# Attention's two column tiles in one step and one bank per l, where a batch's part has at most 256 tokens

## The chip, the cores and the metric

The kernel runs on one core of one Trainium2 chip. The metric is the device time of one execution in microseconds, as the median of several runs. The core's engines are named as the profile names them: PE is the tensor engine (PEld its weight loads), DVE the vector engine, ACT the scalar engine, POOL the GpSimd engine, SP the engine that issues most of the DMAs.

## The reference

A linear attention with a root-mean-square norm is followed by a two-layer network with a leaky ReLU. All data are float32; there are 8 batches of 576 tokens, 8 heads of 64, so 4608 rows of 512 for the network, whose inner width is 2048.

```python
kv = np.einsum('bhsd,bhse->bhde', k, v)
out = np.einsum('bhsd,bhde->bhse', q, kv)
rms = np.sqrt(np.mean(out * out, axis=-1, keepdims=True) + 1e-06)
attn_out = (out / rms * g_norm).astype(np.float32)

B, H, S, D = attn_out.shape                       # 8, 8, 576, 64
x = attn_out.transpose(0, 2, 1, 3).reshape(B * S, H * D)

h = x @ w_in                                      # 512 -> 2048
g = np.maximum(0.01 * h, h)
result = (g @ w_out).astype(np.float32)           # 2048 -> 512
```

## The kernel before

The network works in 9 blocks of 512 tokens, and a batch has 576. So batch b gives 512 - 64b tokens to block b and 64(b + 1) tokens to block b + 1: two parts, each with its own "tail" (`o = q kv`, then the norm). The first 512 tokens of batch 0 are made by code of their own at the start. The other fifteen parts go through the functions below. Parts with at most 256 tokens are the second ones of batches 0 to 3 (64, 128, 192, 256) and the first ones of batches 4 to 7 (256, 192, 128, 64).

Heads lie in pairs (`NP` = 4 pairs p, `l` the half of a pair), and a head's 64 output columns are split into two column tiles e of 32. For one e, eight matmuls fill the two tiles `o_ps[0]` and `o_ps[1]`: each uses 64 rows and 32 columns of the tensor engine's array, so eight of them fit beside one another. A float32 matmul is two instructions in the trace. The tile for the sum of squares, `sum0` or `sum1`, takes the squares of the first column tile directly; those of the second go to a buffer of `t2k` and are added.

```python
    ps_att = ctx.enter_context(tc.tile_pool(name="ps_att", bufs=2, space=bass.MemoryType.PSUM))
    ps_m = ctx.enter_context(tc.tile_pool(name="ps_m", bufs=1, space=bass.MemoryType.PSUM))

    pin = tc.keep_in_program_order
    steady = first_done = False

    def in_turn(ins):

        if steady:
            pin(ins)
# ... cut ...
    N2 = NT // 2                 # 256
# ... cut ...
    def t2k(n, name):
        home = {"tag": name, "bufs": 1} if name[:3] == "sum" else {"tag": "t2k", "bufs": 3}
        return work.tile([P, n], F32, name=name, **home)

    def x_of(lo, hi):
        return block(lo // NT)[:, :, lo % NT:lo % NT + hi - lo]

    def o_products(b, lo, hi, e, o_ps):
        for p in range(NP):
            for l in range(2):
                r = slice(64 * l, 64 * l + 64)
                matmul(o_ps[half_of(p, l)][E * p:E * p + E, :],
                       lhsT=kvs[b % 2][r, p, E * e:E * e + E],
                       rhs=qTs[b][r, p, lo - b * S:hi - b * S], start=True, stop=True)

    def outputs(b, lo, hi, e, sums):


        x, n = x_of(lo, hi), hi - lo
        o_ps = [ps_att.tile([P, n], F32, tag="att", name="o_ps") for _ in range(2)]
        o_products(b, lo, hi, e, o_ps)
        for l in range(2):
            sq = t2k(n, "sq" if e else f"sum{l}")
            nc.scalar.activation(sq, o_ps[l], func=AF.Square)
            if e == 0:
                sums.append(sq)
            else:
                in_turn(nc.vector.tensor_add(sums[l], sums[l], sq))
        for l in range(2):
            nc.scalar.activation(x[:, 2 * l + e, :], o_ps[l], func=AF.Copy, scale=g_sb[:, e:e + 1])
```

The tiles `o_ps` lie in `ps_att`, which has two banks. They are shared with the products of k and v of the next batch. `divide` turns the sums, takes root and reciprocal, spreads them and scales x; it is a generator, so that its pieces can be placed in different slots:

```python
    def divide(lo, hi, sums):

        x, n = x_of(lo, hi), hi - lo
        rms = work.tile([P, 2, n // E], F32, tag="rms", name="rms", bufs=2)
        for l in range(2):
            t = t2k(n, "turned")
            in_turn(nc.vector.transpose(t, sums[l]))
            in_turn(nc.vector.tensor_reduce(rms[:, l, :], t.rearrange("p (a i) -> p a i", i=E),
                                            axis=AX.X, op=ALU.add))
            if l:
                act = nc.scalar.activation(rms, rms, func=AF.Sqrt, scale=1.0 / D, bias=eps_sb)
                if first_done:
                    pin(act)
            yield
        in_turn(nc.vector.reciprocal(rms, rms))
        spread = []
        for l in range(2):
            t = t2k(n, "spread")
            nc.scalar.copy(t.rearrange("p (a i) -> p a i", i=E),
                           rms[:, l, :].unsqueeze(2).to_broadcast([P, n // E, E]))
            spread.append(t)
        yield
        for l in range(2):
            inv = t2k(n, "inv")
            in_turn(nc.vector.transpose(inv, spread[l]))
            to = x[:, 2 * l:2 * l + 2, :]
            in_turn(nc.vector.tensor_mul(to, to, inv.unsqueeze(1).to_broadcast([P, 2, n])))
            yield

    def tail_of(b, lo, hi, fine=False):
        sums = []
        for e in range(2):
            outputs(b, lo, hi, e, sums)
            yield
        for _ in divide(lo, hi, sums):
            if fine:
                yield
        if not fine:
```

From the third block on (`fine`), the steps of one batch are dealt out over the slots of a block's network, and the second part's first column tile comes between two pieces of the first part's norm:

```python
        # in attention(b, apart, fine): the two parts of a batch
        tails = [tail_of(b, max(i * NT, b * S), min((i + 1) * NT, (b + 1) * S), fine)
                 for i in (b, b + 1)]
        if not fine:
            for tail in tails:
                yield from tail
            return

        for tail in (0, 0, 0, 0, 0, 1, 0, 0, 1, 1, 1, 1, 1, 1):
            next(tails[tail])
            yield
```

The network's products are made by Strassen's method in seven steps. A slot has one step of the first product (`h_ha` and `h_hb`, or `h_hc` and `h_hd`, 8 + 6 matmul instructions), then what attention has for this slot, then one step of the second product (`o_a` or `o_c`, 8 instructions). Banks of `h` are added to and emptied in turn, so that a step writes a bank only after the scalar or the vector engine has taken out the one before it:

```python
            for t in range(7):
                slot = 7 * c + t
                go(h_steps, 1)
                if not one:
                    # ... cut ...
                    for _ in range(FINE_SLOTS.get(slot, 0)):
                        go(a_steps, 1)
                    # ... cut ...
                if slot in HELD and i == NB - 1:
                    pass
                elif waited == LAG:
                    go_o()
```

In the steps of block 2 and later (`steady`), the instructions of the vector engine go through `in_turn` and keep the order in which they are written; so do all matmuls, always. Those of the scalar engine may be put in another order when the program is built.

Of the kernel before, what the change touches and what calls it, by code (L numbers as in the profile page):

```python
# [9 lines left out]
F32 = mybir.dt.float32  # L10
U32 = mybir.dt.uint32
I64 = mybir.dt.int64
AF = mybir.ActivationFunctionType
# [10 lines left out]
def kernel(  # L24
# [36 lines left out]
    nc = tc.nc  # L61
    B, H, S, D = q.shape
    DM, DF = w_in.shape
    P = 128
# [7 lines left out]
    N2 = NT // 2  # L72
# [14 lines left out]
    ps_att = ctx.enter_context(tc.tile_pool(name="ps_att", bufs=2, space=bass.MemoryType.PSUM))  # L87
# [5 lines left out]
# [4 lines that stand above are left out]
# [20 lines left out]
    def matmul(*args, **kw):  # L117
        pin(nc.tensor.matmul(*args, **kw))  # L118
# [4 lines left out]
    def half_of(p, i):  # L123


        return i ^ (p & 1)
# [168 lines left out]
    g_sb = consts.tile([P, 2], F32, name="g_sb")  # L295
# [6 lines left out]
    def block(i):  # L302
        if i not in xTs:
            xTs[i] = xpool.tile([P, NE, NT], F32, tag="xT", name="xT")
        return xTs[i]
# [20 lines left out]
# [57 lines that stand above are left out]
            in_turn(nc.vector.tensor_mul(to, to, inv.unsqueeze(1).to_broadcast([P, 2, n])))  # L383
            yield

    def tail_of(b, lo, hi, fine=False):
        sums = []
        for e in range(2):
            outputs(b, lo, hi, e, sums)
            yield  # L390
        for _ in divide(lo, hi, sums):
            if fine:
                yield
        if not fine:
            yield

    def attention(b, apart=True, fine=False):
# [31 lines left out]
        if not apart:  # L429
            copy_kv(b, kv_ps)  # L430
# [4 lines that stand above are left out]
# [488 lines left out]

    first_attention()
    steps = {i: tail for tail in [tail_of(0, NT, S)] for i in (6, 8, 10)}
    a_steps = attention(1, False)
    steps.update((i, a_steps)
# [21 lines left out]
    x_sides, _, sums, _ = sides_x(1)  # L949
# [27 lines left out]
    for i in range(1, NB):  # L977
# [4 lines left out]
        for c in range(NC):  # L982
# [3 lines left out]
# [4 lines that stand above are left out]
# [7 lines left out]
                    if i + 1 < NB:  # L997
                        if slot == 20:
                            x_sides, new_quarters, sums, inner = sides_x(i + 1)
# [13 lines left out]
                if one:  # L1013
# [14 lines left out]
                    if slot == 24:  # L1028
                        go(a_steps)
                        x_sides, new_quarters, sums, inner = sides_x(i + 1)  # L1030
# [47 lines left out]
```

## Time and profile before

| what | value |
|---|---|
| median of 3 runs | 932.22 us (930.87 to 932.27) |
| span of the profiled run | 929.0 us, 17587 instructions |
| granted PE clock in the profiled run | 0.999 |
| o_ps matmuls on PE | x544, of these x64 at the start |
| Square into `sum` and `sq` on ACT | x30 and x30 |
| copies of o_ps into xT on ACT | x60 |
| additions of `sum` and `sq` on DVE | x30 |

The profile's page begins with each engine's busy time, its share of the span and its number of instructions. The chain that ended last is followed back from the last instruction, at each step to what released it; asked for in order of time, it lists start, length and what ran. In a list of waits each line has who waited, for whom, the total in us, how often, and the longest. In the timeline a line has start, length, engine, line of the code, operation, output and inputs, shape and count, and in brackets the idle time ahead of it. Some lines of the timeline name a helper: L118 is every matmul but a few, so there the tile's name tells what it is.

### The profile page before, as it was taken

How to read it: one execution, taken by the hardware profiler on the slowest of the kernel's cores; microseconds unless marked ns; L12 is line 12 of the kernel's file. 1: busy time of each engine (PE TensorE's matmuls, PEld its weight loads, DVE VectorE, ACT ScalarE, POOL GpSimd, SP SyncE). 2: the span in 40 equal slices, each digit the busy share in tenths (PEclk: the TensorE clock that was granted, in tenths of full speed). 3: DMA queues.
4: the chain of work that ended last, by engine and by line, in shares of the span. 5: the costliest groups of instructions: out<-in, count | busy, mean ns of one | idle time of the engine just before them, and what ended most of it. 6: DMA issues, size and time to landing. Idle time of an engine off the chain costs nothing.

```text
span 929.0 us, 17587 instructions
## 1 busy us (share of the span) xinstructions
PE 918.4 (99%) x6856; PEld 776.2 (84%) x6856; DVE 619.2 (67%) x998; ACT 331.0 (36%) x667; POOL 319.0 (34%) x318
## 2 busy tenths in 40 slices
PE   8999999999999999999999999999999999999997
PEld 5544447888998999899989999899988999999996
DVE  4866995586456876597756874687568744654554
ACT  4544632242134332532343423342343333223330
POOL 2000364977522532226211711272225322532222
PEclk9999999999999999999999999999999999999999
DMA  9999926895597679856995599658655676667632
GB/s 258 226 246 239 217 99 199 275 298 165 193 323 245 184 206 300 267 175 190 284 289 180 172 281 293 202 179 256 229 168 177 197 219 185 186 199 221 189 111 91
DMA packets 90066, 200.03 MB, mean 215 GB/s; under 512 B 9856, under 2 KB 42112, under 8 KB 89984
## 3 DMA queue, kind: packets, MB, share of 16 engines
q1 hardware_dynamic: 79392, 186.85, 68.5%
q10 hardware_dynamic: 10144, 10.88, 3.4%
q8 instruction: 55, 0.90, 0.4%
q0 software_dynamic: 448, 1.18, 0.3%
q14 instruction: 27, 0.22, 0.1%
HBM read 172.39 MB, written 26.48 MB: 214 GB/s over the span
## 4 chain that ended last, share of the span: by engine, by line
PE 95%; DMA 2%; DVE 2%; issue 0%; ACT 0%; POOL 0%; ACTq 0%; DVEq 0%; POOLq 0%
PE o_a L118 21%; PE o_c L118 21%; PE h_ha L118 11%; PE h_hb L118 8%; PE h_hc L118 8%; PE h_hd L118 6%; PE o_acc L118 6%; PE h_ps L118 6%; PE o_ps L118 2%; PE kv_ps L118 2%; PE h_a L118 1%; PE h_b L118 1%; DMA pairs<-in_v_dram 1%; PE h_c L118 1%; PE h_d L118 1%; DMA pairs<-in_moe_w_out_dram 1%
## 5 line engine op out<-in xcount | busy, mean ns | idle before, releaser
L589 POOL TENSOR_TENSOR gs<-g 128x512 f32<-128x512 f32 x64 | 81.3, 1289 | 442.9 <-ACT g L760 442.9
L589 DVE TENSOR_TENSOR o<-o_c,o 128x512 f32<-128x512 f32 x104 | 71.6, 689 | 111.8 <-PE o_c L118 111.8
L760 ACT ACTIVATE g<-g 128x512 f32<-128x512 f32 x124 | 78.2, 631 | 120.5 <-DVE g L589 120.5
L824 ACT COPY w_all<-h_ha 128x512 f32<-128x512 f32 x84 | 48.7, 580 | 187.9 <-PE h_ha L118 179.2
L589 DVE TENSOR_TENSOR o<-o_a,o 128x512 f32<-128x512 f32 x88 | 60.5, 687 | 68.0 <-PE o_a L118 67.9
L118 PE MATMUL o_c<-pairs,gs 128*128 128x256 f32 x384 | 91.3, 381 | 0.0
L118 PE MATMUL o_a<-pairs,gs 128*128 128x256 f32 x384 | 90.8, 379 | 0.0
L118 PEld LDWEIGHTS o_c<-pairs,gs 128*128 128x128 f32 x384 | 69.8, 190 | 9.3 <-issue 1.4
L118 PEld LDWEIGHTS o_a<-pairs,gs 128*128 128x128 f32 x384 | 69.8, 190 | 7.8
L118 PE MATMUL o_c<-w,g 128*128 128x256 f32 x256 | 61.6, 383 | 0.0
L118 PE MATMUL o_a<-w,g 128*128 128x256 f32 x256 | 61.6, 383 | 0.0
L118 PEld LDWEIGHTS h_ha<-stage,w_all 128*128 128x128 f32 x448 | 58.7, 192 | 2.8
L118 PE MATMUL h_ha<-stage,w_all 128*128 128x128 f32 x448 | 59.0, 275 | 0.0
L118 PE MATMUL h_ps<-xT,w_all 128*128 128x512 f32 (+1 forms) x136 | 57.9, 570 | 0.2 <-DVE w_all L255 0.2
L118 PE MATMUL o_acc<-w,g 128*128 128x512 f32 x128 | 58.0, 597 | 0.0
L589 DVE TENSOR_TENSOR g<-g,pairs 128x512 f32<-128x512 f32 x84 | 55.6, 689 | 1.9
L118 PEld LDWEIGHTS o_a<-w,g 128*128 128x128 f32 x256 | 46.4, 190 | 11.4 <-ACT pairs L824 2.7
L589 POOL TENSOR_TENSOR pairs<-w_all 128x512 f32<-128x512 f32 x8 | 11.1, 1386 | 123.3 <-DMA stage<-in_moe_w_in_dram 95.4
L118 PEld LDWEIGHTS o_c<-w,g 128*128 128x128 f32 x256 | 46.4, 190 | 5.8
L118 PEld LDWEIGHTS h_ps<-xT,w_all 128*128 128x128 f32 x136 | 25.5, 190 | 29.2 <-issue 26.5
L589 DVE TENSOR_TENSOR g<-w_all 128x512 f32<-128x512 f32 x28 | 21.8, 780 | 40.9 <-ACT w_all L824 40.9
L589 DVE TENSOR_TENSOR w_all<-h_hc,w_all 128x512 f32<-128x512 f32 x56 | 38.4, 686 | 15.3 <-PE h_hc L118 15.0
(193 smaller groups left out, 2039.3 us busy)
## 6 DMA issues: line engine op xcount, KB each, us to landing
w_all<-w SPq DMA_DIRECT2D x196, 448.0 KB, 4.1
pairs<-w SPq DMA_DIRECT2D x56, 512.0 KB, 4.4
out_dram<-o ACTq DMA_DIRECT2D x36, 256.0 KB, 4.6
v_in<-in_v_dram SPq DMA_DIRECT2D x29, 288.0 KB, 5.6
k_in<-in_k_dram SPq DMA_DIRECT2D x28, 288.0 KB, 5.8
q_in<-in_q_dram SPq DMA_DIRECT2D x56, 144.0 KB, 6.4
q_in<-in_q_dram SPq DMA_DIRECT2D x56, 140.0 KB, 6.3
w<-stage SPq DMA_DIRECT2D x12, 512.0 KB, 4.6
```

Of the source, the lines that this page charges most:

```text
L118: pin(nc.tensor.matmul(*args, **kw))
L589: ins = eng.tensor_tensor(out_, a, b_, op=ALU.subtract if minus else ALU.add)
L760: nc.scalar.activation(t, t if src is None else src, func=AF.Prelu, alpha=SLOPE)
L824: nc.scalar.copy(q[:, at], banks[tag])
```

## The change

Where a part has at most 256 tokens, both column tiles fit side by side into one bank (2 x 256 float32 columns). The changed kernel makes them so: `o_ps[l]` has the shape [128, 2, n], all 32 matmul instructions of the part come in one step, one Square per l takes both column tiles, and the vector engine adds its two halves into `sum`. The second step of such a part is then empty, so that the pieces after it keep their slots. Parts of more than 256 tokens go as before. It is meant to save scalar-engine instructions, and to have the small matmuls of a part in one go.

```diff
--- before.py
+++ after.py
@@ -383,11 +383,32 @@
             in_turn(nc.vector.tensor_mul(to, to, inv.unsqueeze(1).to_broadcast([P, 2, n])))
             yield
 
+    def both_outputs(b, lo, hi, sums):
+
+        x, n = x_of(lo, hi), hi - lo
+        o_ps = [ps_att.tile([P, 2, n], F32, tag="att", name="o_ps") for _ in range(2)]
+        for e in range(2):
+            o_products(b, lo, hi, e, [o[:, e, :] for o in o_ps])
+        for l in range(2):
+            sq = t2k(2 * n, "sq").rearrange("p (e n) -> p e n", e=2)
+            nc.scalar.activation(sq, o_ps[l], func=AF.Square)
+            sums.append(t2k(n, f"sum{l}"))
+            in_turn(nc.vector.tensor_add(sums[l], sq[:, 0, :], sq[:, 1, :]))
+        for l in range(2):
+            for e in range(2):
+                nc.scalar.activation(x[:, 2 * l + e, :], o_ps[l][:, e, :], func=AF.Copy,
+                                     scale=g_sb[:, e:e + 1])
+
     def tail_of(b, lo, hi, fine=False):
         sums = []
-        for e in range(2):
-            outputs(b, lo, hi, e, sums)
+        if hi - lo <= N2:
+            both_outputs(b, lo, hi, sums)
             yield
+            yield
+        else:
+            for e in range(2):
+                outputs(b, lo, hi, e, sums)
+                yield
         for _ in divide(lo, hi, sums):
             if fine:
                 yield
```

## The prediction

> **What bounds the kernel now.** I read the page first: busy shares and the shares of the chain that ended last.
>
> ```profile
> PE 918.4 (99%) x6856; PEld 776.2 (84%) x6856; DVE 619.2 (67%) x998; ACT 331.0 (36%) x667; POOL 319.0 (34%) x318
> ...
> PE 95%; DMA 2%; DVE 2%; issue 0%; ACT 0%; POOL 0%; ACTq 0%; DVEq 0%; POOLq 0%
> ```
>
> The tensor engine is busy 99% of the 929.0 us, and 95% of the chain runs through it; the rest of the chain is the start. [...]the second view is the list of waits of the tensor engine alone:
>
> ```profile
> PE idle_ps L118 <- DVE group L291: 1.5, 1, 1.5
> PE o_ps L118 <- issue: 1.1, 1, 1.1
> PE inv_ps L118 <- DVE roots L542: 0.8, 2, 0.4
> ...
> PE h_b L118 <- ACT g L785: 0.5, 1, 0.5
> ```
>
> All the waits of the list add up to 5.7 us, and only the last of these four lies after the start. So almost nothing that the vector, scalar or GpSimd engine does ends a wait of the tensor engine, and a saving on those three is worth nothing unless it lets matmuls start sooner. What counts is how long the tensor engine's own work takes, switches between kinds of work included. For that I read the chain in order of time, in a stretch with a part that the change touches (256 tokens; start, length, what):
>
> ```profile
> 373.96 0.67 PE h_hd L118 x6
> 374.63 0.59 PE o_ps L118 x16
> 375.22 1.92 PE o_c L118 x8
> 377.15 0.89 PE h_ha L118 x8
> 378.04 0.67 PE h_hb L118 x6
> 378.71 1.73 PE o_a L118 x8
> ...
> 384.62 0.67 PE h_hd L118 x6
> 385.29 0.59 PE o_ps L118 x16
> 385.88 1.92 PE o_a L118 x8
> ```
>
> A slot without attention is 0.89 + 0.67 + 1.73 = 3.29 us. A slot with one column tile has 0.59 us more for it, and the eight matmuls after it take 1.92 in place of 1.73 us: 0.19 us is lost on the way back to full-size tiles. The two column tiles of the same part stand 10.66 us apart (374.63 and 385.29), so that this is paid twice. How much of the 0.59 is paid per visit shows in the smallest and the largest part:
>
> ```profile
> 669.50 0.27 PE o_ps L118 x16
> 669.77 1.92 PE o_c L118 x8
> ...
> 707.84 1.02 PE o_ps L118 x16
> 708.86 1.92 PE o_a L118 x8
> ```
>
> 64 columns take 0.27 us, 512 take 1.02 us, with the same 16 instructions. The slope is 0.75 / 448 = 1.674 ns per column; the rest is 0.27 - 64 x 0.00167 = 0.163 us per visit. The line through these two gives 0.59 for 256, which is what the chain has. With the 0.19 us afterwards a visit costs 0.163 + 0.19 = 0.35 us beside its columns, whatever its width.
>
> [...]The attention's matmuls use 64*32 tiles and the blocks around them 128*128[...]. In the changed step row half l of pair p still writes the bank that it wrote before, for both column tiles[...]. [...]the trace's Square has 388 ns at 256 and 594 at 512, that is 0.80 ns per column and some 180 ns fixed.
>
> **The change part by part.** Which parts: batch b has 512 - 64b tokens in block b and 64(b+1) in block b+1. At most 256 are 64, 128, 192, 256 (b = 0 to 3, the second part) and 256, 192, 128, 64 (b = 4 to 7, the first part): eight of the fifteen parts that take this path. The other seven keep their two visits.
>
> 1. Tensor engine. The 16 + 16 matmul instructions of a part come in one visit. Columns and instructions are the same, and one visit of two is gone: 0.35 us per part, 8 x 0.353 = 2.8 us. A joint visit for 256 tokens should look like today's 512-column visit, 1.02 us, and 1.92 us after it. That no cost hides between the two column tiles is seen in the first attention, where both tiles of both halves run in one go: rows of eight instructions with 256 columns start at 17.81, 18.02, 18.24 and 18.45 us, 0.215 us apart, and the slope above makes 8 of 16 instructions 256 x 1.674 / 2 = 0.214 us. For 64 columns 32 instructions may be held by their issue: the visits for k and v do 72 instructions with 64 columns in 1.21 us, 16.8 ns each. If that were the pace, a joint visit of 64 took 0.54 us, and such a part saved 0.19 in place of 0.35 us. There are two of them; I take off 0.1 us for this. Sum: 2.7 us, all of it on the path that sets the end.
>
> 2. Scalar engine. Four Squares become two of twice the width: 16 fewer instructions at about 180 ns, 2.9 us of busy time. Four copies stay four. This lies beside the tensor engine, which doesn't wait for it: worth nothing by itself.
>
> 3. Vector engine. Still two additions per part, of the same width, but in the earlier visit's slot and not in the place of the second. At the second visit of a first part (386.40 us) two additions of 256 columns took 1.93 us while GpSimd summed g at the same time; in the earlier slot the vector engine idles for 3.5 us before 378.75 us and GpSimd is idle too. There I expect about 0.45 us each (the transpose of 256 columns has 0.43). Again beside the path.
>
> 4. Buffers. Squares take two of the three "t2k" buffers for up to 512 columns. For the first parts nothing else uses them at that point. For batch 3's second part (256 tokens) the two spread tiles of the part before are still alive, so its second Square must wait for the first addition; the scalar engine loses perhaps 1 us there, once.
>
> **The rivals.** (A) The doubled evacuation is late, and the tensor engine waits for a bank. Scalar engine in the same slot (start, length, what):
>
> ```profile
> 375.31 0.66 ACT L349 ACTIVATE sum<-o_ps 128x256 f32<-128x256 f32 x2 [1.62 <-PE o_ps L118]
> 375.86 0.84 ACT L355 ACTIVATE xT<-o_ps,g_sb 128x256 f32<-128x256 f32 x2
> ...
> 378.07 0.59 ACT L824 COPY w_all<-h_ha 128x512 f32<-128x512 f32 x1 [0.30 <-PE h_ha L118]
> 378.75 0.48 ACT L824 COPY pairs<-h_hb 128x384 f32<-128x384 f32 x1
> ```
>
> h_ha is written again from 380.44 us in the chain, 1.8 us after its copy ends. In the joint step the Squares start 0.43 us later, at 375.74, take 1.1 us, and the four copies 1.7 us: 378.5. Then come the copy of o_c (0.59), of h_ha and of h_hb: 379.1, 379.7, 380.1. The matmuls that need them have also moved by 0.43, to 380.87 and 381.76. About 1.2 us of room is left, and less width leaves more. If the order on the scalar engine came out worse, a stall of some 0.5 us in the four slots of batches 4 to 7 would eat 2 us: about no change. (B) The 0.35 us isn't per visit but per instruction, and nothing is saved; against it speak the even rows of the first attention. (C) The vector engine, which keeps the written order, stands at the head of its queue for Squares twice as long (0.59 for 0.39 us), and its additions into h and o come later. They have holes of 1 to 5 us ahead of them in these slots; worth 0 to 0.5 us. (D) The freed scalar and vector time shortens the kernel beyond the 2.7 us: the waits list has nothing that it could shorten.
>
> **Range and chances.** 932.2 - 2.7 = 929.5 us. The three times of before span 1.4 us, which a median of a few runs carries along, and (A) and (C) could give back up to 2.5 us, while nothing could bring much more than 3: 927.8 to 931.4. A 2% change would be 18.6 us, seven times the sum; only an unlucky order of the instructions over many slots could cost so much. Faster by over 2%: 0.005; within: 0.98; slower: 0.015.
>
> **What would show it right or wrong.** Right: the span falls by 2.5 to 3 us, with eight visits of o_ps x32 in the chain, 1.02 us at 256 and near 0.38 to 0.54 at 64, eight fewer groups of 1.92 us, and no new wait of the tensor engine. Squares up to 128x512 number 16 fewer; the additions of batches 4 to 7 are near 0.45 us or less. Wrong: visits of x32 that take as long as two, or a new wait of an h or o matmul for the scalar or the vector engine just after a joint step. A median above 932 would mean that (A) or (C) is more than I make of it.

## The result and the profile after

In the first comparison the changed kernel's median was 927.36 us (926.41 to 929.14, 6 runs), beside 931.05 us of the kernel before (929.50 to 932.27, 6 runs): a ratio of 0.9964, with a 95% interval of 0.9949 to 0.9978. That is faster, well within 2%, and 0.44 us below the predicted range. With the later comparisons there are 42 runs of the changed kernel, median 929.0 us, and 147 of the kernel before, median 931.7 us: 0.997 of it.

The tensor engine still sets the time. The page of the changed kernel (busy times, then the chain by engine):

```profile
PE 915.1 (99%) x6856; PEld 776.5 (84%) x6856; DVE 615.5 (67%) x998; ACT 328.7 (36%) x651; POOL 317.6 (34%) x318
...
PE 95%; DMA 2%; DVE 2%; issue 0%; ACT 0%; POOL 0%; SPq 0%; ACTq 0%; DVEq 0%; POOLq 0%
```

The number of matmul instructions is the same; 16 instructions are gone on the scalar engine, with 2.3 us of its busy time. The chain in order of time shows batch 4's part with 256 tokens (start, length in us, what):

```profile
372.63 0.67 PE h_hd L118 x6
373.30 1.02 PE o_ps L118 x32
374.33 1.92 PE o_c L118 x8
...
383.72 0.67 PE h_hd L118 x6
384.39 1.73 PE o_a L118 x8
```

One visit of 32 instructions takes 1.02 us where two took 0.59 each, and the slot that held the second visit has none now: its o_a takes 1.73 in place of 1.92 us. The narrowest part, 64 tokens, and the widest one, which is unchanged, later in the same view:

```profile
667.10 0.38 PE o_ps L118 x32
667.49 1.92 PE o_c L118 x8
...
684.13 1.02 PE o_ps L118 x16
685.15 1.92 PE o_a L118 x8
```

0.38 us for 64 tokens where two visits took 0.27 each. The tensor engine's waits:

```profile
PE o_ps L118 <- issue: 1.7, 1, 1.7
PE idle_ps L118 <- DVE group L291: 1.5, 1, 1.5
...
PE h_b L118 <- ACT g L806: 0.4, 1, 0.4
```

The wait of h_b was there before (0.5 us); no wait for an h or an o bank has come after the joint visits. The wait at the head of the list stands at the start, and will be of use below.

From the start of the network's first matmul to that of its last one, the instruction records give 896.96 us for the kernel before and 894.27 us after: 2.69 us. The spans differ by 3.5 us (929.0 and 925.5). The rest of that is 0.1 us ahead of this stretch and 0.7 us after the last addition, 4.13 us before and 3.41 us after. Laid side by side, one matmul of the network after the other, the records also show where the 2.69 us lie: at each of the eight parts the changed kernel gains 0.355 to 0.362 us, with 64 tokens as with 256. Between the parts the two keep step, but for one visit for k and v that took 0.17 us longer in the changed kernel.

### The profile page after: what moved, and what is told of

Its sections match the earlier page's. It is cut to its first block, busy times and chain, and to the rows that moved or that the text cites. A ratio compares the mean times of both kernels' runs of the same rounds, so it can differ in the third digit from the quotient of the medians.

```text
span 925.5 us, 17566 instructions
## 1 busy us (share of the span) xinstructions
PE 915.1 (99%) x6856; PEld 776.5 (84%) x6856; DVE 615.5 (67%) x998; ACT 328.7 (36%) x651; POOL 317.6 (34%) x318
## 4 chain that ended last, share of the span: by engine, by line
PE 95%; DMA 2%; DVE 2%; issue 0%; ACT 0%; POOL 0%; SPq 0%; ACTq 0%; DVEq 0%; POOLq 0%
PE o_a L118 21%; PE o_c L118 21%; PE h_ha L118 11%; PE h_hb L118 8%; PE h_hc L118 8%; PE h_hd L118 6%; PE o_acc L118 6%; PE h_ps L118 6%; PE o_ps L118 2%; PE kv_ps L118 2%; PE h_a L118 1%; PE h_b L118 1%; DMA pairs<-in_v_dram 1%; PE h_c L118 1%; PE h_d L118 1%; DMA pairs<-in_moe_w_in_dram 1%
## 5 line engine op out<-in xcount | busy, mean ns | idle before, releaser
L118 PEld LDWEIGHTS o_acc<-w,g 128*128 128x128 f32 x128 | 24.0, 190 | 29.8 <-issue 29.4
```

## The experiments

Theory V: the visits alone are the gain, a visit being one stay of the tensor engine with small tiles between full ones. The rivals were the scalar engine's 16 instructions (S), the place of the additions (G), and, for the 0.7 us at the end, an end of the changed kernel's own (E).

**Both kernels again, unchanged.**

> The kernel before, once more, unchanged. Theory V says that the change is worth eight visits of the small tiles, 2.75 us, and that what the first comparison had beyond it (0.7 us of span after the last addition, and a median of before that moved from 932.2 to 931.05 us) is chance. Then this run agrees with the runs of before: ratio 1.000 with an interval of about 0.001 to either side, medians between 930 and 932 us, and the stretch from the last addition on the vector engine to the end of the span may be anything from 3.3 to 4.3 us, where the first two profiles had 4.13 and 3.42 us. Rival E (the changed kernel ends sooner for a reason of its own, such as its stores): the stretch is 4.1 us again here, as in the first profile of before.

> The changed kernel, once more, unchanged. Theory V: ratio to before near 1 - 2.75 / 931 = 0.9970, between 0.9960 and 0.9980; the stretch from the last addition to the end of the span differs from the 3.42 us of the first profile. Rival E: ratio 0.9963 or less, and the stretch is 3.4 us again.

The kernel before gave 932.02 us and a ratio of 1.000 (0.9988 to 1.0011); the changed one 928.8 us and 0.9954 (0.9939 to 0.9969). The stretch of the network was 896.96 us again for the one, and 894.09 us for the other: 2.87 us less, and in the profiles of one and the same kernel it doesn't move by more than 0.2 us. The first profile of the changed kernel had the 0.17 us longer visit for k and v. After the last addition the kernel before now took 3.41 us. So rival E falls: 4.1 and 3.4 us come up with either kernel.

**One bank and half the Squares, but two visits.**

```diff
         for e in range(2):
             o_products(b, lo, hi, e, [o[:, e, :] for o in o_ps])
+            if e == 0:
+                yield
# ... cut: in tail_of ...
-            both_outputs(b, lo, hi, sums)
-            yield
+            yield from both_outputs(b, lo, hi, sums)
             yield
```

> One bank per l, one Square for both column tiles and half as many Squares, as in the changed kernel, but the second column tile's matmuls stay in the step in which the kernel before has them: sixteen visits in place of eight. Theory V (the visits are all): the whole gain is gone, ratio 0.999 to 1.001, about 931 us. Rival S (the 16 scalar instructions spared are what counts): ratio 0.997, as the changed kernel. Rival G (it is the additions' place, away from GpSimd's sums): as V, for the additions are again in the later step; the next run tells V from G.

932.2 us, ratio 1.0005 (0.9994 to 1.0017), and 896.94 us in the stretch. The chain of this kernel:

```profile
375.37 0.59 PE o_ps L118 x16
375.96 1.92 PE o_c L118 x8
...
386.02 0.59 PE o_ps L118 x16
386.62 1.92 PE o_a L118 x8
```

The scalar engine has its 651 instructions, as in the changed kernel, and nothing is gained: S falls.

**One visit, but a Square for each column tile.**

```diff
-        for l in range(2):
-            sq = t2k(2 * n, "sq").rearrange("p (e n) -> p e n", e=2)
-            nc.scalar.activation(sq, o_ps[l], func=AF.Square)
-            sums.append(t2k(n, f"sum{l}"))
-            in_turn(nc.vector.tensor_add(sums[l], sq[:, 0, :], sq[:, 1, :]))
+        for e in range(2):
+            for l in range(2):
+                sq = t2k(n, "sq" if e else f"sum{l}")
+                nc.scalar.activation(sq, o_ps[l][:, e, :], func=AF.Square)
+                if e == 0:
+                    sums.append(sq)
+                else:
+                    in_turn(nc.vector.tensor_add(sums[l], sums[l], sq))
```

> One visit and one bank per l, as in the changed kernel, but a Square for each column tile, the first ones into the sum tiles as in the kernel before: 60 Squares again, and the scalar engine busy about 2.5 us longer than in the changed kernel. Theory V: ratio 0.997, the same as the changed kernel within 0.001. Rival S: ratio 1.000. Rival G: as V, since the additions stay in the early step.

928.94 us, ratio 0.9967 (0.9955 to 0.9979), with 667 scalar instructions. The stretch is 894.66 us. The 0.57 us over the 894.09 of the changed kernel's second profile lies in the first slots of block 2, where two experiments below that have no such Squares lose time too (six_held 0.56 us, two_held 1.0 us); why it comes and goes was not tried. This run doesn't tell V from G: the additions stay in the early slot. The first two traces do. In batch 1's second part (128 tokens) the early slot put the two additions where GpSimd is at work (five instructions without a gap from 132.09 to 137.39 us), and they take longer there; first the kernel before, then the changed one:

```profile
138.88 0.46 DVE L353 TENSOR_TENSOR sum<-sum,sq 128x128 f32<-128x128 f32 x2
```

```profile
134.13 1.54 DVE L396 TENSOR_TENSOR sum<-sq 128x128 f32<-128x128 f32 x2
```

Yet this part gained 0.359 us like the other seven: G falls.

**The limit at 128 tokens.** `if hi - lo <= P` in place of `<= N2`.

> The changed kernel with its limit at 128 tokens in place of 256: only four of the eight parts (64, 128, 128, 64) are made in one visit, the two of 192 and the two of 256 go back to two. Theory V: half the gain, 4 x 0.359 = 1.44 us less than the kernel before between the first and the last matmul of the network (895.5 us, where before has 896.96 and the changed kernel 894.1 to 894.3); ratio near 0.9985. Rival W (the gain goes with the columns that are joined): these four parts have 384 of the 1280 columns, so 0.86 us of the gain, 896.1 us.

930.47 us, ratio 0.9984 (0.9975 to 0.9994). The stretch is 895.52 us, 1.44 us less than before and 1.43 us more than the changed kernel's 894.09: exactly half the gain for half the parts, although they have 30% of the columns. W falls.

**More visits for k and v.** If a visit costs the same whatever it does, splitting those for k times v must cost as much. The first edit had the second half a step later, and the loads after it:

```diff
-            attention_kv(b, m, kv_ps)
+            attention_kv(b, m, kv_ps, range(5) if apart else range(9))
+            if apart:
+                yield
+                attention_kv(b, m, kv_ps, range(5, 9))
# ... cut ...
```

> The changed kernel, but for batches 2 to 7 each of the two visits for k and v is split into two (5 and 4 of the 9 row groups), the second one a step later: twelve more visits with the same matmuls in all. Theory V (a visit costs 0.35 us, whatever it does): 12 x 0.36 = 4.3 us more between the network's first and last matmul, 898.4 us in place of 894.1; a little more if the smaller 64*64 tiles cost more per visit (0.44 us from their 1.21 us for 72 instructions: 5.3 us, 899.4). Ratio to before about 1.0015 to 1.003. Rival P (what was saved is peculiar to the two column tiles in one bank): no change, 894.1 us.

It took 967.02 us, ratio 1.0381 (1.0362 to 1.0399), and says nothing of visits. Its waits:

```profile
PE kv_ps L118 <- DMA v_in<-in_v_dram: 22.9, 6, 10.7
```

The halves hold their buffers for a step longer, so the next pairs come later, and the tensor engine waits up to 10.7 us for v. The second edit leaves the loads where they were and puts the second half after the second product's step of the same slot:

```diff
+            attention_kv(b, m, kv_ps, range(5) if fine else range(9))
+            if fine:
+                later.append((b, m, kv_ps, range(5, 9)))
# ... cut: after go_o() of the slot ...
+                while later:
+                    attention_kv(*later.pop())
```

> The first try to split the visits for k and v moved loads, and the tensor engine then waited for them. Here, for batches 3 to 7 in the changed kernel, four of the nine row groups of each such visit come just after the second product's step of the same slot, and the loads stay where they were: ten more visits with the same matmuls. Theory V (every visit costs 0.35 to 0.44 us, whatever it does): 10 times that more between the network's first and last matmul, 897.6 to 898.5 us in place of 894.1, ratio to before 1.0005 to 1.0025. Rival P (what the change saved is peculiar to the two column tiles in one bank): 894.1 us.

932.42 us, ratio to the kernel before 1.0014 (1.0003 to 1.0024), and 897.65 us in the stretch: 3.55 us over the 894.10 of the changed kernel, 0.355 us for each of ten visits. One slot of it in the chain:

```profile
239.56 0.74 PE kv_ps L118 x40
240.30 1.92 PE o_c L118 x8
242.23 0.62 PE kv_ps L118 x32
242.85 1.09 PE h_hc L118 x8
```

The halves take 0.74 + 0.62 = 1.36 us where the whole took 1.21, and what comes after the second one takes 1.09 in place of 0.89 us. The additions into sum are where the changed kernel has them, so G can't explain this: a visit costs 0.355 us with these matmuls as with those of q and kv.

**Where the runs differ.** The network's stretch is steady to 0.2 us in the profiles of either kernel, yet the runs of the kernel before spread from 929.2 to 935.5 us. The profiles differ at the start. There the tensor engine stops amid the first attention's o_ps matmuls for nothing that the waits name; the timeline of the kernel with four Squares has the longest stop of the first six profiles:

```profile
15.30 1.17 PE L118 MATMUL o_ps<-qT,kv 64*32 64x256 f32 x27 [0.52 <-DVE kv L321]
19.27 1.71 PE L118 MATMUL o_ps<-qT,kv 64*32 64x256 f32 x37 [2.80 <-issue]
20.91 3.33 PE L118 MATMUL sum_ps<-sq,group 128*32 128x256 f32 x12
```

Afterwards the same 12 sum_ps matmuls take 3.33 us, where they take 1.93 after a stop of 1.04 us. The busy times by stretch, first of the kernel before in its second profile, then of this one (us, then PE, PEld, DVE, ACT, POOL busy and the number of instructions, the granted clock, the DMA share, GB/s):

```profile
15.00:20.00 5.00, 3.44 (x84) 2.03 (x78) 1.75 (x6) 2.58 (x5) 0.00 (x0) 1.00 1.03 244
20.00:25.00 5.00, 3.95 (x51) 2.36 (x48) 3.44 (x8) 1.78 (x5) 0.00 (x0) 1.00 1.10 226
```

```profile
15.00:20.00 5.00, 1.90 (x59) 1.35 (x62) 0.77 (x3) 1.26 (x3) 0.00 (x0) 1.00 1.01 239
20.00:25.00 5.00, 4.78 (x37) 2.43 (x21) 2.80 (x7) 2.56 (x5) 0.00 (x0) 0.66 1.06 231
```

The clock falls to 0.66 in the mean after the longer stop; its own records show one half for 3.41 us. In all 14 traces the records of the clock lie on a grid of 3.41 us: the changed kernel's first one, for example, is at full clock for 921.60 us, 270 windows of 3.413 us. Of all windows within the runs, those that a lowering followed, 12 in number, had the tensor engine idle for 1.81 to 2.71 us; in every other one at full clock it was idle for 1.79 us or less (the runs' last microseconds, where its work ends, left aside). So in these traces 1.81 us in one window was enough, and it matters how a stop lies: the 2.11 us of bank_two_visits fell into two windows, 0.51 and 1.60, and nothing was lowered, while 2.09 us in one window of kv_in_two lowered the clock.

The mean clock is known for 141 of the 147 runs of the kernel before and for all 42 of the changed one, and it sorts them: 75 runs of the kernel before with 0.999 or 1.000 have a median of 930.5 us, 66 with 0.998 or less 932.5 us; of the changed kernel 23 have 927.9 and 19 have 929.9 us. Between the kernels the difference is 2.65 us on both sides.

What stops it? The first guess was four loads of weights, issued from 15.3 us on. They were held by a copy of the first Square into their places:

```diff
-        for j in range(3, 7):
-            load_w(j)
# ... cut: after the first Square ...
+                pin(nc.scalar.copy(pairs.rearrange("p (i n) -> p i n", i=4)[:, :, :32],
+                                   squares[0][0].rearrange("p e (i n) -> p (e i) n", i=2)[:, :, :32]))
+                for j in range(3, 7):
+                    load_w(j)
```

> About the spread that moves the whole time, not about the change. In every profile so far the tensor engine stops for 1.0 to 2.8 us in the middle of the first attention's o_ps matmuls, after 27 of 64 instructions, waiting for nothing that the profile shows, and the network's first matmul starts at 26.7 to 29.7 us. Four loads of weights are issued just then, at about 15.3 us. Here they are held back until the first Square is done, by a copy of the Square's output into their places, 3 to 4 us later. Theory F (the tensor engine's own instructions come late since these loads stand before them): the stop shrinks to under 0.7 us, the network's first matmul starts at 25.3 to 26.5 us, and the median falls 1 to 3 us below the changed kernel's, ratio to before 0.993 to 0.996. Rival Q (the stop has nothing to do with these loads): the stop stays at 1 to 3 us, and the time is that of the changed kernel or longer, since the weights come later.

The guess was wrong: the stop was 3.15 us, the network began at 30.6 us, and the median was 930.41 us, ratio 0.9984 (0.9971 to 0.9997). But the DMA records show a transfer of 16,384 bytes on an instruction queue ahead of every stop. The page of the changed kernel has two queues of this kind (packets, MB, share of the DMA engines):

```profile
q8 instruction: 55, 0.90, 0.4%
...
q14 instruction: 27, 0.22, 0.1%
```

All 55 transfers of q8 have 16,384 bytes. Which engine's instructions they are, the trace doesn't say. An estimate from its numbers: q8 moved 80% of the 1.12 MB of the two queues, and the tensor engine has 14,051 of the trace's 17,566 records, 80% too, so q8 is likely its queue; the expectations that follow take it for that. The stop comes before the same matmul, the 28th of the 64, in all 13 profiles that have one, and ends 2.4 to 3.0 us after the transfer's start. So next six loads were held, the two issued at 12.7 to 13.7 us among them, first until the scalar engine had worked on weight 0 (about 17.5 us), then only until k times v was copied (about 15.1 us), each time by a small copy into the places of weights 1 and 2; the second edit:

```diff
         copy_kv(0, kv_ps)
+        pin(nc.vector.tensor_copy(stage.rearrange("p (i n) -> p i n", i=3)[:, 1:, :32],
+                                  ident[:, :64].rearrange("p (i n) -> p i n", i=2)))
+        for j in range(1, 7):
+            load_w(j)
```

> Holding four loads did nothing for the stop (it was 3.15 us). But in all eight profiles so far it ends 2.7 to 3.0 us after a 16 KB transfer of the tensor engine's instructions starts, at 14.9 to 16.4 us, and the loads of two other weights are issued just before that, at 13.7 us. Here the loads of weights 1 to 6 are all held until the first weight's pieces have gone through the scalar engine, at about 17.5 us. Theory F2 (the instructions' transfer stands behind those two loads): it starts before 14.6 us, the stop is under 0.7 us and ends before 17.2 us, the clock isn't lowered at the start, and the network's first matmul starts at 25 to 26.5 us; if the later weights still come in time, the median is 1 to 2.5 us below the changed kernel's, with fewer runs at a clock of 0.998 or less. Rival Q2 (the transfer is asked for only then, by the tensor engine's own progress): it starts 1 to 3 us after the last k and v products have started, as before, the stop stays over 1 us, and the time is that of the changed kernel or longer.

> The changed kernel, unchanged, beside it on the same chip: ratio to before 0.9955 to 0.9975, and 894.0 to 894.4 us between the network's first and last matmul, whatever the start does. Runs at a clock of 0.999 or 1.000 near 927.3 us, runs at 0.998 near 929.5 us, as the runs of before fall near 930.4 and 932.6 us.

> As in the last run but one, but the loads of weights 1 to 6 wait only for the vector engine's copies of k times v (about 15.1 us), so that the two loads of 13.7 us come 1.5 to 2 us later and the other four about when they did. Theory F2: the transfer of the tensor engine's instructions starts near 14.2 us, the stop is near 0.7 us, the network's first matmul starts near 25.5 us and the clock isn't lowered, and now the weights come in time: 894.1 to 894.5 us between the network's first and last matmul (not 901.9). Then the median is 1 to 3 us below the changed kernel's beside it, ratio to before 0.9935 to 0.996, and few runs are at a clock of 0.998 or less. Rival Q2: no better than the changed kernel.

> The changed kernel, unchanged, beside it: ratio to before 0.9965 to 0.998, 894.0 to 894.4 us between the network's first and last matmul.

All in us, from the profiles; the stop is the idle time between the two groups of o_ps matmuls:

| profile | instruction transfer starts | stop | o_ps goes on | network starts | network, first to last matmul |
|---|---|---|---|---|---|
| before | 14.94 | 1.13 | 17.81 | 26.78 | 896.96 |
| same_before | 15.15 | 1.04 | 17.95 | 26.93 | 896.96 |
| after | 15.08 | 1.68 | 17.74 | 26.71 | 894.27 |
| same_after | 15.36 | 2.16 | 18.28 | 28.73 | 894.09 |
| bank_two_visits | 15.60 | 2.11 | 18.55 | 27.53 | 896.94 |
| visit_four_squares | 16.37 | 2.80 | 19.27 | 29.73 | 894.66 |
| up_to_128 | 15.26 | 2.71 | 18.29 | 28.75 | 895.52 |
| kv_in_two | 15.20 | 2.09 | 17.86 | 28.31 | 932.37 |
| kv_around | 15.14 | 0.97 | 17.81 | 26.79 | 897.65 |
| weights_held | 16.10 | 3.15 | 18.91 | 30.60 | 894.22 |
| six_held | 14.16 | 0.68 | 16.52 | 25.50 | 901.86 |
| two_held | 14.45 | none | - | 25.79 | 905.04 |
| after_beside | 15.59 | 1.71 | 18.27 | 27.24 | 894.10 |
| after_beside_2 | 15.02 | 1.78 | 17.62 | 26.60 | 894.10 |

With six loads out of the way the transfer starts at 14.16 and 14.45 us, in the other twelve profiles at 14.94 to 16.37, and the stop shrinks to 0.68 us or goes. The tensor engine's own progress also moves, though. From the start of its last 72 matmuls for k and v to the transfer it is 1.28 us in six_held and 0.57 in two_held, beside 1.20 to 3.43 in the others, so only two_held stands apart by this measure, with one profile: that the loads ahead delay the transfer is likely and not shown. In two_held's timeline all 64 instructions are one group:

```profile
15.67 2.63 PE L118 MATMUL o_ps<-qT,kv 64*32 64x256 f32 x64 [0.51 <-DVE kv L321]
18.23 1.93 PE L118 MATMUL sum_ps<-sq,group 128*32 128x256 f32 x12
```

Yet neither is shown to beat the changed kernel. Six_held gave 929.55 us, ratio 0.9993 (0.9972 to 1.0014), beside 929.25 us, 0.9977 (0.9970 to 0.9984), of the changed kernel; two_held gave 936.99 us, 1.0058 (1.0045 to 1.0071), beside 929.87 us, 0.9978 (0.9968 to 0.9988). In two_held the weights come too late, for the DMA engines have time to spare meanwhile (their share is the last but one number) and are full afterwards; below that are its waits:

```profile
15.00:20.00 5.00, 4.49 (x88) 2.46 (x80) 2.91 (x10) 3.21 (x6) 0.00 (x0) 1.00 0.55 124
20.00:25.00 5.00, 3.53 (x53) 2.50 (x56) 2.82 (x7) 2.44 (x7) 0.00 (x0) 1.00 1.10 242
```

```profile
PE h_ps L118 <- DVE w_all L255: 2.9, 5, 0.7
PE kv_ps L118 <- DMA v_in<-in_v_dram: 2.5, 1, 2.5
```

So two_held loses 10.9 us: 9.6 of them in the network's first block, where the clock also stood at one half for 6.8 us, and 1.0 at the start of block 2. The expectation that the weights would be in time was wrong. For six_held the table shows a slower run (933.69 us). Seven of its 14 runs had a clock of 0.999 or 1.000, with a median of 928.05 us beside 928.28 us of the changed kernel's nine such runs; whether its weights are late in those too isn't known. Nothing that was tried is shown to be faster than the changed kernel.

## Why the prediction was right or wrong

**Step 1, the visits: right.** The predicted 2.7 us were 2.69 and 2.87 us in the network's stretch of the two pairs of profiles, and 1.44 us for half of the parts. That the first of these is so close is luck: it has the 0.17 us longer visit in it. Eight visits alone are 2.86 us, beside 2.8 in the prediction's sum ahead of its allowance. The cost per visit, predicted from the 64 and the 512 column visits as 0.353 us, was 0.355 us when ten were added. The 256 token visit took the 1.02 us that today's 512 column visit had. Only the allowance of 0.1 us for 64 tokens wasn't needed (by its own figures it would have been 2 x 0.16): the joint visit took 0.38 us, not 0.54. The pace of the k and v matmuls, 16.8 ns each, doesn't hold for these 64*32 tiles: 32 in 0.38 us are 11.9 ns each. What the cost of a visit consists of, no run here shows.

**Step 2, the scalar engine: right.** 16 instructions fewer, 2.3 us of busy time instead of the predicted 2.9, and worth nothing by themselves, as the run with two visits shows.

**Step 3, the additions: right for batches 4 to 7.** In the early slot, with GpSimd idle, the two of batch 4 take 0.43 us each:

```profile
375.06 0.92 DVE L396 TENSOR_TENSOR sum<-sq 128x256 f32<-128x256 f32 x2 [1.16 <-ACT sq L394]
```

They took 1.93 us together in the later one. For batches 1 and 2 the early slot isn't the quiet one: 0.81 us each with 128 columns where it was 0.26, and 2.2 us together with 192 columns where it was 2.3. No gain or loss came of either.

**Step 4, the buffers: right, and without a cost.** For batch 3's second part the second Square does come after the first addition, 1.2 us after the first Square; the program put two of the copies between them, so the scalar engine lost nothing.

**Rival A, the late evacuation: it didn't come.** The scalar engine after batch 4's joint visit:

```profile
374.43 1.08 ACT L394 ACTIVATE sq<-o_ps 128x512 f32<-128x512 f32 x2 [2.07 <-PE o_ps L118]
375.40 1.57 ACT L399 ACTIVATE xT<-o_ps,g_sb 128x256 f32<-128x256 f32 x4
376.83 0.62 ACT L879 COPY o<-o_c 128x512 f32<-128x512 f32 x1
377.29 0.64 ACT L845 COPY w_all<-h_ha 128x512 f32<-128x512 f32 x1
377.85 0.48 ACT L845 COPY pairs<-h_hb 128x384 f32<-128x384 f32 x1
```

The visit begins 1.33 us earlier here than in the kernel before (373.30 for 374.63). With that taken off, the predicted times were 374.4 for the first Square and 378.8 for the end of the h_hb copy (its terms add up to 0.1 more); they are 374.43 and 378.33. h_ha is written again at 379.54, 1.6 us after its copy ended; 1.2 had been predicted. Rivals B, C and D didn't come either: eight times 0.357 us leave nothing for them.

**What failed is the step under "Range and chances": "932.2 - 2.7 = 929.5 us", its first term and the width around it.** In the first comparison the kernel before had 931.05 us where 932.2 had been put, and the difference there was 3.7 us, 1 us more than the stretch of the network can give. These two, 1.15 and 1.0 us, make the 2.1 us from 929.5 to 927.36; either alone would have stayed inside the 1.7 us down to 927.8. The prediction took three runs that span 1.4 us for all that the start and the end can do. They do more: in the profiles without any change at the start the network starts at 26.6 to 29.7 us, and the end takes 3.4 or 4.1 us; 147 runs of the kernel before span 6.3 us. The first six runs of the changed kernel were low ones by luck: five of them had a mean clock of 0.999 or 1.000, as had 18 of the 36 later ones. The later three comparisons gave 928.8, 929.25 and 929.87 us, and all 42 runs 929.0 us. This much is shown: the size of the change is as predicted, and in the four profiled runs of the changed kernel, of 927.0 to 929.1 us, the spread lies outside the part that it touches. Its slower runs, up to 931.1 us, have no trace. How the starts and ends of the first six runs fell out isn't known run by run, for only one of them has a trace.

## What to carry to other kernels

Where the tensor engine is the bound, count the changes between small and full tiles, not only the matmuls: here each stay with small tiles cost 0.355 us beside its columns, so what can be done in one stay should be, and instructions spared on an engine that isn't waited for were worth nothing. Read a small gain from a stretch between two fixed instructions of the trace, which was steady to 0.2 us in the profiles of one kernel here, and not from whole times, which spread over 6 us. Before giving a range in whole microseconds, ask which parts of the span differ from run to run; three runs don't show it.

## What the runs showed of the hardware

- A stay with small tiles cost 0.355 to 0.362 us beside its columns: eight were taken away with 64*32 tiles (64 to 256 columns), ten added with 64*64 tiles (64 columns).
- In 13 of 14 profiles the tensor engine stopped for 0.68 to 3.15 us amid small matmuls, and the stop ended 2.4 to 3.0 us after the start of a transfer of 16,384 bytes on an instruction queue, by the estimate above the tensor engine's. In the one profile of two_held, with six loads held back, there was no stop, and the time still wasn't better (936.99 us beside 929.87).
- In the 14 traces, the runs' ends left aside, the clock went from full to one half after the 12 windows of 3.41 us in which the tensor engine idled for 1.81 to 2.71 us, and after none with 1.79 us or less. Twelve matmuls that take 1.93 us together then took up to 3.50 us (weights_held).
- Two additions of 256 columns on the vector engine took 0.92 us while GpSimd was idle and 1.93 us while it summed.
